# Equal token blocks in the second part of an MLP: five of 460 or 464 tokens in place of four of 512 and one of 256

## The chip, the cores and the metric

The kernel runs on one core of one Trainium2 chip. The metric is the device time of one execution in microseconds (us). The engines are TensorE (PE, with its weight loads shown apart as PEld), VectorE (DVE), ScalarE (ACT), GpSimd (POOL) and SyncE (SP, which issues the DMAs).

## The reference

Three layers follow each other over 2304 tokens (4 batches of 576) of 512 features, all in float32.

```python
x = attention(q, k, v, M_prev, z_prev, beta)       # (2304, 512), 8 heads of 64, causal, mixed with a memory read
h = x @ w_in                                       # first MLP: 512 -> 2048
g = s * relu(h)**2 + b
x = g @ w_out                                      # 2048 -> 512
h = x @ w2_in                                      # second MLP: 512 -> 1024
e = softmax(h) * h
ln = (e - mean(e)) / sqrt(var(e) + 1e-6) * g_ln
return ln @ w2_out                                 # 1024 -> 512
```

## The kernel before

**Arithmetic.** The float32 operands of the MLPs are split into a high and a low part of type fp32r, and each product of two matrices is made of three matmuls: high by high, high by low, low by high. Tokens are the moving operand in the first MLP, so the column count of a matmul is a number of tokens; the weights, 128 by 128, are the stationary operand, and each matmul has a weight load of its own.

**Stages.** The 16 groups of 128 hidden units of the first MLP (`f`, FF = 2048) are split. The first 4 groups (`FP1`) are done by `first_part`, in blocks of `NB` = 512 tokens (the last of 256), woven into the attention; its result goes to the DRAM tile `yd`. The other 12 groups (`FP2`) are done by `second_part` after the attention. The second MLP (`mlp2`) ends the kernel, 256 tokens at a time.

**second_part.** The line `blocks = ...` cuts the 2304 tokens into five blocks (t0, n). A round is one block with six of the groups: `rounds` holds the five blocks with groups 4 to 9, then the five blocks with groups 10 to 15, so ten rounds. Groups are taken two at a time, in three pairs for each round. For a pair, `hidden2` computes the hidden values with a Winograd form of the 2x2 block product: seven products (`product`, line 1098, into the PSUM tiles X, Y, V, W), each of six matmuls on m = n // 2 tokens; that is 42 matmuls of m columns for a pair and 126 for a round. Between the products ACT and DVE combine the results (lines 1123 to 1142), then `gate_of` squares and scales them on n columns (lines 1115 to 1119). `y2` (lines 1155 to 1157) multiplies by `w_out`: 12 matmuls of n columns for a group, 72 for a round; at the sixth group the sum is added into `yT` in SBUF (line 1161).

**What a round needs.** `forms2` makes the seven Winograd forms of the block, each as a high and a low tile, from x: POOL makes the differences (lines 968 to 976), ACT takes the high part (961), DVE the low part (962). There is one buffer for each form. In rounds 0 to 4 the forms are also written to the DRAM tile `fd` (line 965, 14 DMAs a round); rounds 5 to 9 read them back (line 953, 14 DMAs). `load2` brings x and the sums of `first_part` for the next round. Beside this the weights are decoded on ACT, DVE and POOL (`decode_to`), by a count of steps, three in a round.

**Order.** The program is traced loop by loop, but the order in which each engine runs its instructions is written out by hand in the dictionary `ORDER`: for each engine a list of the instructions' numbers in the order of tracing (`a+n` means n in a row from a). PE's list weaves the products of a pair with the matmuls of `y2` of the pair before, so that PE has work while the other engines handle a product. `SLOTS` names the buffer of each tile.

Of the kernel before, what the change touches and what calls it, by code (L numbers as in the profile page):

```python
# [50 lines left out]
1366+2 1428+3 1368+2 1420+8 1388+6 1387 1462 1445 1406+2 1431 1463+4 1446 1432+10 1394+4 1442+2 1398+2 1467 1447  # L51
1453+4 1448+2 1468+4 1461 1472+2 1450+3 1444 1491+12 1457 1474+2 1458 1476 1459+2 1477 1516+9 1478+7 1503+8 1485+2
1511+2 1487+4 1513+3 1540+2 1528 1525 1529 1526 1530+6 1542 1536+2 1543+2 1538+2 1545+5 1552+2 1550+2 1554+2 1527
1556+2 1564 1558 1565+4 1559 1569+2 1560+3 1571 1563 1572+9 1624 1588 1625+2 1589 1627 1636 1628+2 1637+3 1630
1640+5 1631+2 1645+2 1633 1647 1581+2 1590 1634+2 1591 1660+2 1583 1662+3 1648+2 1592 1650 1665 1584 1651 1593 1585
1594 1586+2 1652 1666 1653+2 1595+3 1600+2 1598+2 1602+9 1667 1612 1655 1613 1611 1656 1668 1614 1669 1657+3 1670
1615+2 1671+2 1617+7 1673+12 1726 1685 1720 1686+4 1696 1690+2 1697+2 1721 1692+2 1699 1694 1700+2 1695 1702+6
1722+3 1708+3 1727 1711+2 1728 1713 1729 1714+3 1725 1717+3 1730 1738+5 1744+6 1743 1731+7 1762 1768+2 1763+3 1756+5
1750 1761 1751+5 1766 1770 1767 1771+2 1774+4 1780+2 1773 1782 1778 1783 1779 1784 1789+2 1785 1791+4 1807+6 1795
1813 1796 1804+2 1814 1786 1815 1787 1797 1867 1816+5 1868 1798 1821 1799+2 1822 1801+3 1823+3 1828+2 1826 1830 1827  # L60
1831+2 1834+2 1843+2 1833 1836 1845 1837+3 1806 1861+4 1849 1858 1846 1865 1788 1840 1866 1869 1859 1841 1850 1852+6
1860 1847+2 1876 1851 1906 1842 1915+3 1894+3 1918 1907+2 1879 1873 1909 1897+2 1919 1910 1874+2 1911 1899 1870 1880
1900 1871 1885 1901+5 1920 1924 1877 1925+2 1881 1927 1966+5 1872 1878 1928 1936 1888 1929 1948+2 1937+2 1950 1939
1951+3 1940 1971 1960+2 1941 1882 1972+2 1962+2 1974 1964 1891 1975 1965 1976 1978 1892 1886+2 1883 1977 1987 1884
1889 1979 2020 1893 1890 2005 1988 2006 1980 2007 1981 2021 1989 2008+2 1982 1990 2022 1991 2010 1992 1983 2023
1933+2 2024 1912 2025 1996+4 2014 2000 2015 2001 2016+2 2026 2018 2027 2019 1935 2028 1921 2032 2029 1922 2030 2041
2031 1923 1930 1913 1931 1945 2042 1946 1957+2 1932 1914 1959 1954 1947 1955+2 1942+3 2059+2 2033+2 2061 2035 2062+2
2043 2036+2 2044+2 2064 2046 1993 2011 1994+2 2092+2 2002 2050+2 2094 2052+2 2095 2104 2054 2105 2096 2055 2106+2
2097 2047 2108 1984+2 2113 2122 2114+2 2109 2116+2 2048 1986 2003+2 2012 2056 2038 2013 2065 2039+2 2057 2066+2 2098
2058 2049 2099+5 2123 2068 2124 2069 2118 2164 2125 2165+2 2146+3 2167 2149 2126+2 2168+2 2150 2134 2151 2135+3 2070  # L70
2138+2 2158+3 2170 2161+3 2171 2176 2172+2 2177 2071 2178 2185+4 2072 2074 2174+2 2179 2075 2073 2083 2218 2076+3
2203 2079 2086 2089 2087 2090 2080 2091 2084 2088 2081 2085 2082 2180 2204 2219+4 2205+3 2181 2223 2208 2189+2
2128+2 2119+2 2212+3 2121 2194+6 2224 2215+2 2225+3 2217 2230+2 2131 2110 2228 2239 2232 2143 2132 2240+2 2233 2111
2133 2112 2130 2140 2152+3 2144 2229 2141 2155 2145 2156 2142 2157 2234 2200 2242 2191 2243 2257 2192+2 2258+2 2235
2260+2 2201+2 2244 2262 2254 2209 2248 2182 2249 2302 2183 2303 2250+3 2245 2253 2246 2290 2304 2291+2 2184 2293
2305 2311+2 2294 2313 2306 2295 2210 2314+2 2236 2255 2237+2 2296 2211 2316 2320 2256 2297 2247 2263+2 2298 2265
2321 2299 2322 2300+2 2272 2323+2 2307 2275 2266 2362 2273 2269 2325 2344 2274 2363 2345 2364 2346 2270 2347 2365
2271 2348 2366+2 2281 2332 2349 2282 2333 2267 2334 2356 2335+2 2357+2 2337 2359+2 2368+2 2268 2370+2 2361 2374+2
2276 2278 2376+2 2277 2378 2372 2287 2373 2284 2383 2379 2384 2279 2285 2385+2 2286 2401 2288 2283 2280 2387+2 2289
2308 2402 2309 2403 2326+2 2317 2410 2310 2318 2411 2328 2412 2404 2338+2 2319 2392 2341 2393 2350 2394 2340 2329  # L80
2342 2351 2343 2352 2330+2 2353+3 2395+2 2380 2397+2 2405 2416 2406 2417 2413+2 2389+2 2399 2407 2381 2415 2382 2391
2408 2400 2409 2418+28 2461 2455 2462 2452+2 2456+4 2463 2473 2467 2454 2468 2470 2446 2460 2447 2474 2471 2448 2464
2475 2449+3 2465+2 2472 2488+2 2469 2482 2485 2483 2490 2486+2 2509 2500 2510 2479 2511 2476+2 2512 2480 2484 2478
2491+2 2506+2 2501 2481 2502 2527 2493 2515 2524 2503 2513 2516 2504 2514 2517 2508 2528 2494 2525 2518 2495+5 2519
2505 2529 2520 2551 2536 2521+3 2526 2548 2560+3 2539 2530+6 2554+2 2542 2549 2552 2543+3 2572 2546+2 2563 2556 2537
2564 2557 2540 2558+2 2541 2566 2573 2567 2565 2553 2574 2568 2550 2569 2575 2538 2581 2570+2 2582+2 2614 2576
2615+2 2584+2 2599 2577 2600+2 2586 2602+2 2617 2596 2604+2 2618+2 2587 2578 2608+2 2590 2610 2591+4 2611+2 2595
2620+4 2613 2624 2579 2606 2625 2588+2 2580 2626+2 2635 2628 2636+2 2629 2638 2632 2639 2692 2653 2630 2640 2631
2654+3 2607 2659 2597 2657 2660 2693 2658 2644 2694 2633 2645+3 2641 2648+2 2642 2695 2598 2696 2634 2650 2662 2643
2697+3 2686 2700 2687 2701 2707 2688+3 2661 2691 2702 2708+3 2703 2665 2651 2716 2671 2711 2758 2652 2717 2712  # L90
2718+2 2663 2759+2 2720 2664 2740 2721 2741+4 2761 2745 2674 2752 2666 2753 2762 2668 2672 2667 2763 2677 2764 2754
2765 2755 2766+2 2728 2756 2768 2729+4 2757 2733 2769 2678+2 2669+2 2673 2779 2680 2770 2780 2681 2781 2771 2683+2
2682 2675 2685 2676 2797+2 2772 2782 2773 2799 2783+2 2713 2800 2774 2801 2775 2802 2725 2722 2704+2 2726 2714
2788+4 2818 2706 2812+2 2792 2819 2814+2 2820 2793 2816+2 2734 2715 2821 2806 2824 2807+4 2822 2737 2811 2823 2727
2749 2738 2735 2739 2723+2 2736 2833 2746 2750+2 2747+2 2825 2834 2826+3 2835 2890 2803 2836 2891 2829 2837 2851+2
2838 2853 2892 2854+2 2785 2856 2893 2776 2842+3 2777 2845+3 2896 2778 2894 2884+3 2897 2887 2794 2895 2888 2830
2898 2786 2889 2787 2795 2899+3 2804+2 2956 2839 2796 2840 2848 2957 2905 2841 2849 2958 2906 2831 2907 2850 2959+2
2914+2 2832 2857 2916 2858+2 2917 2908+2 2918 2938 2919 2910 2961 2860+2 2869 2939+2 2950 2863 2951 2941+3 2870 2952
2871 2926+2 2953 2928+4 2962 2954+2 2963+2 2864 2968+2 2965 2866 2977+2 2970 2867 2966 3010 2868 2862 2979 3011 2980
2865 3012 2971+2 2981 3013 2967 2973 3014 2878 2982 3015 2881 2995+2 2875+2 2882 2877 2872+2 3004 2997 2879+2 2883  # L100
2874 3005 2998 2902 2999 3006 2911 3007 2912 3008+2 2920 2923 3000 2903 2924 2913 2921 2925 3016+2 2986+4 3018
2990+2 2947 2935 3019 2948 3022 3020 3023 2949 3021 3031 2936+2 2922 2904 3088 3032 2944 2932+2 2945 2934 2946 3033
3089 3034+2 3090 3036 3024+2 3049+2 3026 3091 3051+4 3027 3092 2983 3001 2992 3082+4 3002 3086 3040+5 2984 3045 3094
3003 3093 3095+3 2974 3087 3098+2 2985 2975 2993 3055 2994 3056 3046+2 3037 3103+3 2976 3038 3028 3112 3154 3039
3029 3057 3030 3048 3155+2 3113 3106 3157 3114 3158 3115 3058 3136 3116 3107 3064 3117 3059 3061 3108 3137+3 3159
3060 3140 3124 3062 3125+2 3141 3067 3127+3 3148 3070 3160+2 3149+2 3162 3065 3068 3151 3166 3152+2 3163 3069 3079
3063 3175 3071 3066 3167 3073 3076 3074 3164 3208 3080 3075 3165 3072 3209 3077 3176+3 3168 3078 3081 3169 3210 3193
3179 3194 3109 3211+2 3170 3195+2 3180 3171 3121+2 3213 3197 3202+2 3198 3123 3204+4 3184+6 3100 3214+2 3101 3216
3220 3110+2 3217 3221+2 3218 3229+3 3219 3286+2 3102 3223 3118 3133 3288 3145+2 3119 3247 3120 3147 3248 3130 3289
3131 3134 3132 3135 3142+3 3232 3290 3224 3249 3233 3225 3250+2 3234 3172 3199 3291 3173 3200 3252 3201 3280+4 3174  # L110
3181 3292+2 3190 3294+2 3238+3 3284 3241 3296 3242+2 3297 3182 3285 3226 3191 3301 3227 3310 3302 3253 3303 3352+2
# [1269 lines left out]
```

## Time and profile before

| what | value |
|---|---|
| time, median of 3 runs (lowest to highest) | 807.01 us (805.99 to 808.16) |
| the profiled execution: its time, and the span in its trace | 806.04 us, 804.3 us |
| PE busy | 794.9 us (99% of the span) |
| DVE, ACT, POOL busy | 604.4, 567.7, 157.0 us |
| granted TensorE clock, mean | 0.999 |

The span runs from the first to the last instruction of the trace; the time has some 1.7 us around it. PE's busy time counts overlapping matmuls once, and the ends of matmuls are modelled, so the length of a matmul is read from the distance between the starts of neighbours and not from its duration. The times in the rows are us from the span's start, and durations of single instructions are ns where a row says mean.

### The profile page before, as it was taken

What the parts mean: (1) busy time and instruction counts of PE and PEld (TensorE: products, weight loads), DVE (VectorE), ACT (ScalarE), POOL (GpSimd) and SP (SyncE); (2) the same over time, 40 slices, a digit from 0 to 9 for tenths busy, and PEclk for the clock granted to TensorE, in tenths of its full rate; (3) what the DMA queues carried; (4) which work ended last, traced back from release to release, by engine and by line L of the source; (5) the groups of instructions that cost most, each with busy time, mean ns of one, the idle gap of its engine ahead of it and who ended that gap; (6) DMA issues with size and microseconds to landing.
All of it is one profiled execution on the core that took longest, in us unless ns stands there. A gap on an engine that the chain in (4) does not pass through costs nothing.

```text
span 804.3 us, 15061 instructions
## 1 busy us (share of the span) xinstructions
PE 794.9 (99%) x5406; PEld 666.4 (83%) x5406; DVE 604.4 (75%) x1486; ACT 567.7 (71%) x1189; POOL 157.0 (20%) x170
## 2 busy tenths in 40 slices
PE   9999999999999999999999999999999999999997
PEld 6777777877777898988899888989987888888886
DVE  6999988878789886877577579765689756766751
ACT  7999988888797669886588677765856445545542
POOL 3221232121001524221121002500012212222000
PEclk9999999999999999999999999999999999999999
DMA  8463572545766568881769867467782000001001
GB/s 262 144 206 97 161 215 80 167 151 183 253 166 189 176 214 267 279 284 52 241 236 312 290 236 261 149 233 244 242 320 90 35 13 27 28 14 40 26 14 66
DMA packets 69167, 134.02 MB, mean 167 GB/s; under 512 B 9484, under 2 KB 26596, under 8 KB 69092
## 3 DMA queue, kind: packets, MB, share of 16 engines
q1 hardware_dynamic: 69092, 133.05, 50.5%
q8 instruction: 43, 0.70, 0.4%
q14 instruction: 32, 0.26, 0.1%
HBM read 91.24 MB, written 41.79 MB: 165 GB/s over the span
## 4 chain that ended last, share of the span: by engine, by line
PE 89%; DVE 5%; ACT 3%; issue 1%; DMA 1%; POOL 1%; SPq 0%; DVEq 0%; ACTq 0%; POOLq 0%
PE y L1157 6%; PE y L1156 6%; PE y L1155 6%; PE pp L791 5%; PE W L1098 5%; PE X L1098 5%; PE V L1098 5%; PE s L734 5%; PE po L823 4%; PE o L1308 4%; PE o L1307 4%; PE o L1309 4%; PE Y L1098 2%; PE y L917 2%; PE y L919 2%; PE zt L1298 2%
## 5 line engine op out<-in xcount | busy, mean ns | idle before, releaser
L1155 PE MATMUL y<-g,w 128*128 128x512 f32 (+1 forms) x240 | 84.1, 379 | 0.0
L1156 PE MATMUL y<-g,w 128*128 128x512 f32 (+1 forms) x240 | 83.3, 376 | 0.0
L1157 PE MATMUL y<-g,w 128*128 128x512 f32 (+1 forms) x240 | 81.9, 377 | 0.0
L717 ACT ACTIVATE pr<-pr,mx 128x128 f32<-128x128 f32 (+3 forms) x128 | 71.0, 558 | 4.3 <-DVE mx L750 3.9
L795 ACT ACTIVATE pt<-pp,omg 128x512 f32<-128x512 f32 (+3 forms) x128 | 62.7, 524 | 9.6 <-PE pp L791 8.2
L750 DVE CUSTOM_DVE_ANT_0 pr<-s,big 128x256 f32<-128x256 f32 (+3 forms) x128 | 59.1, 482 | 10.4 <-PE s L734 9.2
L1098 PE MATMUL X<-fhb,w 128*128 128x256 f32 (+1 forms) x240 | 61.8, 277 | 0.0
L1098 PE MATMUL V<-fht,w 128*128 128x256 f32 (+1 forms) x240 | 61.0, 278 | 0.0
L1119 DVE TENSOR_TENSOR g<-r,g 128x512 fp32r<-128x512 f32 (+1 forms) x60 | 39.2, 654 | 22.9 <-ACT r L1118 19.2
L1307 PE MATMUL o<-w,zh 128*128 128x512 f32 x144 | 54.1, 391 | 0.0
L1117 ACT ACTIVATE g<-r,b_sb,s_sb 128x512 fp32r<-128x512 f32 (+1 forms) x60 | 45.8, 767 | 11.7 <-PE y L1157 10.4
L1308 PE MATMUL o<-w,zh 128*128 128x512 f32 x144 | 53.8, 392 | 0.0
L1309 PE MATMUL o<-w,zl 128*128 128x512 f32 x144 | 53.6, 392 | 0.0
L791 PE MATMUL pp<-ident,pr 128*128 128x128 f32 x320 | 50.1, 276 | 1.7 <-ACT pt L795 0.7
L1115 ACT ACTIVATE r<-r 128x512 f32<-128x512 f32 (+1 forms) x60 | 34.5, 582 | 22.9 <-DVE r L1138 13.2
L791 PEld LDWEIGHTS pp<-ident,pr 128*128 128x128 f32 x320 | 37.9, 140 | 13.0 <-ACT pt L795 2.1
L1157 PEld LDWEIGHTS y<-g,w 128*128 128x128 f32 x240 | 44.2, 189 | 5.0
L1156 PEld LDWEIGHTS y<-g,w 128*128 128x128 f32 x240 | 44.3, 189 | 4.6
L628 POOL TENSOR_TENSOR q<-ph,zb 128x640 f32<-128x640 f32 x16 | 25.7, 1608 | 112.1 <-DVE ph L625 86.3
L1098 PEld LDWEIGHTS X<-fhb,w 128*128 128x128 f32 x240 | 44.3, 190 | 2.8 <-ACT r L1135 0.2
L1118 ACT ACTIVATE r<-r,b_sb,s_sb 128x512 f32<-128x512 f32 (+1 forms) x60 | 45.7, 768 | 1.1
L1155 PEld LDWEIGHTS y<-g,w 128*128 128x128 f32 x240 | 43.8, 189 | 3.3
(223 smaller groups left out, 2414.0 us busy)
## 6 DMA issues: line engine op xcount, KB each, us to landing
raw<-in_moe_w_in_dram SPq DMA_DIRECT2D x24, 512.0 KB, 5.7
raw<-in_moe_w_out_dram SPq DMA_DIRECT2D x24, 512.0 KB, 4.3
wd<-wt SPq DMA_DIRECT2D x21, 512.0 KB, 3.1
w<-wd SPq DMA_DIRECT2D x21, 512.0 KB, 4.7
kq<-in_kq_dram SPq DMA_DIRECT2D x16, 608.0 KB, 5.6
RW<-rd SPq DMA_DIRECT2D x24, 288.0 KB, 5.0
q<-in_q_dram SPq DMA_DIRECT2D x16, 320.0 KB, 3.8
v<-in_v_dram SPq DMA_DIRECT2D x16, 320.0 KB, 5.3
```

The lines of the kernel that those rows point to most:

```text
L717: mark[0] = nc.scalar.activation(pr, pr, AF.Exp, bias=mx, scale=-1.0, accum_out=sm).ins
L750: nc.vector.tensor_tensor_reduce(pr, ss[:, j, at[i]:at[i] + n], big[:, CF * P - i * P:CF * P - i * P + n], -scale, FMAX, ALU.add, ALU.min, mx)
L791: nc.tensor.transpose(pp[:, e * n + c * P:e * n + (c + 1) * P], pr[:, c * P:(c + 1) * P], ident)
L795: nc.scalar.activation(p["pt", i // 2][:, j, 0:i + 1, i % 2, :], pp[:, e * n:(e + 1) * n].rearrange("p (c t) -> p c t", t=P), AF.Copy, sca ...
L1098: nc.tensor.matmul(o, wc[a], b[:, i, 0:m], start=(i == 0 and z == 0 and not more), stop=(i == KH - 1 and z == 2), skip_group_check=True)
L1117: nc.scalar.activation(gh, r, AF.Identity, scale=s_sb, bias=b_sb)
L1155: nc.tensor.matmul(o, wc[0], gh, start=(f == fs[0]), stop=False)
L1156: nc.tensor.matmul(o, wc[1], gh, start=False, stop=False)
L1157: nc.tensor.matmul(o, wc[0], gl, start=False, stop=(f == fs[-1]))
L1307: nc.tensor.matmul(oo, zh, w[:, 0], start=(f == 0), stop=False)
L1308: nc.tensor.matmul(oo, zh, w[:, 1], start=False, stop=False)
L1309: nc.tensor.matmul(oo, zl, w[:, 0], start=False, stop=(f == NF2 - 1))
```

## The change

The five blocks of `second_part` become four of 460 tokens and one of 464, where they were 512, 512, 512, 256 and 512. The half blocks, which are the columns of the matmuls of `product`, become 230 or 232, where they were 256 (or 128 in the block of 256 tokens). Nothing else in the program's loops is changed: the number of instructions of each kind stays as it is, and so do the blocks of `first_part`.

```diff
-    blocks = [(0, NB), (NB, NB), (2 * NB, NB), (3 * NB, NT - 4 * NB), (NT - NB, NB)]
+    BT = NT // 5 // 4 * 4
+    blocks = [(i * BT, BT if i < 4 else NT - 4 * BT) for i in range(5)]
```

The lists of `ORDER` are also replaced in part. They hold the same numbers as before. PE's list has 4654 entries: the first 1405 and the last 730 are unchanged, and of those between some 1500 stand more than 5 places from where they stood, the farthest 84. ACT's list has 1008 entries (farthest 55 places), DVE's 1272 (40), SP's 382 (19) and POOL's 170 (4). Two lines of PE's list, as a sample of the kind of change:

```diff
-1366+2 1428+3 1368+2 1420+8 1388+6 1387 1462 1445 1406+2 1431 1463+4 1446 1432+10 1394+4 1442+2 1398+2 1467 1447
...
+1366+2 1428+2 1368 1430 1369 1431 1420+8 1388+6 1462 1387 1463 1445 1464 1406+2 1465+2 1446 1394+2 1432+2 1396+2
...
```

## Rows read from the trace of the kernel before

**Rows 1.** Page, parts 1, 2 and 4: busy time, granted clock by slices, chain that ended last
```profile
PE 794.9 (99%) x5406; PEld 666.4 (83%) x5406; DVE 604.4 (75%) x1486; ACT 567.7 (71%) x1189; POOL 157.0 (20%) x170
...
PEclk9999999999999999999999999999999999999999
...
PE 89%; DVE 5%; ACT 3%; issue 1%; DMA 1%; POOL 1%; SPq 0%; DVEq 0%; ACTq 0%; POOLq 0%
```

**Rows 2.** Windows, second_part: stretch, its length, busy us (x instructions) of each engine, clock, DMA
```profile
289.70:602.00 312.30, 311.57 (x2038) 281.67 (x2037) 223.47 (x445) 225.80 (x411) 55.43 (x52) 1.00 0.72 241
```

**Rows 3.** Windows, the same stretch, instructions of line 1098 alone: PE busy, PEld busy
```profile
289.70:602.00 312.30, 196.62 (x1260) 181.85 (x1260) 1.00 0.72 241
```

**Rows 4.** Groups of instructions by shape: xcount, busy us, mean ns of one, idle before
```profile
L1098 PE MATMUL X<-fhb,w 128*128 128x256 f32 x192 | 50.9, 282 | 0.0
...
L1098 PE MATMUL X<-fhb,w 128*128 128x128 f32 x48 | 10.8, 254 | 0.0
...
L1155 PE MATMUL y<-g,w 128*128 128x512 f32 x192 | 71.4, 401 | 0.0
```

**Rows 5.** Timeline of PE, 256 columns, two apart: start, duration, line, names, stationary, moving, count
```profile
300.06 0.28 PE L1098 MATMUL Y<-fht,w 128*128 128x256 f32 x1
...
300.30 0.28 PE L1098 MATMUL Y<-fht,w 128*128 128x256 f32 x1
```

**Rows 6.** Windows, the longest stretch of 256-column matmuls alone
```profile
559.72:580.30 20.58, 20.58 (x170) 20.32 (x170) 12.17 (x28) 15.74 (x30) 0.00 (x0) 1.00 0.72 237
```

**Rows 7.** Timeline of PE, stretch of 128 columns alone: first and last, 12 apart
```profile
403.94 0.28 PE L1098 MATMUL Y<-fht,w 128*128 128x128 f32 x1
...
405.29 0.27 PE L1098 MATMUL W<-fht,wh 128*128 128x128 f32 x1
```

**Rows 8.** Timeline of PE, two matmuls of 128 columns among 512-column ones
```profile
379.83 0.44 PE L1156 MATMUL y<-g,w 128*128 128x512 f32 x1
380.12 0.22 PE L1098 MATMUL W<-fht,wh 128*128 128x128 f32 x1
380.18 0.27 PE L1098 MATMUL W<-flt,wh 128*128 128x128 f32 x1
380.29 0.45 PE L1155 MATMUL y<-g,w 128*128 128x512 f32 x1
380.57 0.62 PE L1156 MATMUL y<-g,w 128*128 128x512 f32 x2
```

**Rows 9.** Timeline of PEld, the weight loads in the same stretch
```profile
380.12 0.19 PEld L1098 LDWEIGHTS W<-flt,wh 128*128 128x128 f32 x1
380.23 0.19 PEld L1155 LDWEIGHTS y<-g,w 128*128 128x128 f32 x1
380.34 0.42 PEld L1156 LDWEIGHTS y<-g,w 128*128 128x128 f32 x2
```

**Rows 10.** Timeline of PE, 512 columns in second_part: first and next after four
```profile
371.88 0.39 PE L1157 MATMUL y<-g,w 128*128 128x512 f32 x1
...
372.80 0.28 PE L1098 MATMUL W<-flt,wh 128*128 128x256 f32 x1
```

**Rows 11.** Waits of PE in second_part: who waited for whom, us in total, times, longest
```profile
PE Y L1098 <- DVE flt L962: 0.4, 1, 0.4
PE W L1098 <- DVE r L1132: 0.2, 1, 0.2
```

**Rows 12.** Timeline of PE where round 1 begins
```profile
319.65 0.40 PE L1155 MATMUL y<-g,w 128*128 128x512 f32 x1
320.45 0.38 PE L1098 MATMUL Y<-flt,w 128*128 128x256 f32 x1 [0.40 <-DVE flt L962]
```

**Rows 13.** Groups of ACT in second_part by shape, the gate's line 1117
```profile
L1117 ACT ACTIVATE g<-r,b_sb,s_sb 128x512 fp32r<-128x512 f32 x48 | 38.6, 810 | 6.6 <-PE y L1157 5.9
...
L1117 ACT ACTIVATE g<-r,b_sb,s_sb 128x256 fp32r<-128x256 f32 x12 | 7.2, 596 | 5.1 <-PE y L1157 4.4 <-PE V L1098 0.6
```

**Rows 14.** Windows, round 1 of second_part, columns as in rows 2
```profile
318.70:350.00 31.30, 30.76 (x192) 27.00 (x191) 24.78 (x45) 26.51 (x47) 10.23 (x9) 1.00 0.77 266
```

337 rows, old and new, of the table ORDER are left out of this document.

## The prediction

> **What bounds the kernel.** I read the page first, then windows, then the timeline of PE. The page has PE busy for 99% of the span and on 89% of the chain that ended last, at the full granted clock in every slice (2.4 GHz, the higher of its two levels) [rows 1]. So the time is PE's instruction stream, and an edit counts by what it does to that stream. The window over `second_part`, 312.3 us, says the same of the stage that is changed: PE is busy 311.57 us, DVE 223, ACT 226, DMA at 0.72 [rows 2]. PE waited for another engine 0.6 us in all [rows 11]. What must be known, then, is how long PE takes for a matmul of each width. Durations don't tell (254, 282 and 401 ns for 128, 256 and 512 columns [rows 4], since neighbours overlap); the distances of starts do.
>
> **Prices of a matmul.** With 256 columns, starts stand 120 ns apart [rows 5], and in the longest stretch of that width alone 20.58 us / 170 = 121 ns [rows 6]. I take 121. With 512 columns four steps take 0.92 us: 230 ns [rows 10]. With 128 columns twelve steps take 1.35 us: 112.5 ns [rows 7]. From 512 to 256 the price falls by 109 ns, or 0.426 ns a column; from 256 to 128 it falls by only 8.5. So below some width something else sets the step. Rows 8 and 9 show what. Two matmuls of 128 columns follow one of 512: the second is taken up 60 ns after the first (380.12 to 380.18), because its stream is that short, but the next then stands 110 ns on (380.29), and a 512-column matmul behind it is followed after 280 ns and not after 230. The weight loads run through at 380.12, 380.23 and 380.34, 110 ns apart, whatever the width [rows 9]. A narrow matmul thus waits for the load of the next weights; about 112 ns is a floor for each matmul with a load of its own.
>
> The Trainium skill (TensorE: Matmul & The Clock Gate, section LDWEIGHTS) gives a load of P columns P / 1.2 ns, 106.7 ns for 128 columns; the 110 ns in rows 9 bear the floor out, a little higher. By the page's figure the floor would lie under the stream of 230 columns, the stream would set the step, and the saving worked out below would be an estimated 10 us.
>
> **Removed and added on PE.** Counts first. Line 1098 has 1260 matmuls in the stage [rows 3]; the groups show 192 to 48 for the two widths [rows 4], so 1008 of 256 columns and 252 of 128. `y2` has 720: 576 of 512 and 144 of 256. A check of the prices: 1008 x 0.121 + 252 x 0.1125 = 150.3 us, and 576 x 0.230 + 144 x 0.121 = 149.9 us. PE ran 2038 matmuls in the stretch; the other 58 belong to the neighbouring stages, at 0.121 to 0.230 us another 7 to 13 us. The sum, 307 to 313, is the stage's 312.3.
>
> *Products.* After the change all 1260 have 230 columns (252 of them 232). No row has that width. The line through 256 and 512 columns gives 121 - 26 x 0.426 = 110 ns, under the floor of 112.5, so I take 112.5: 1260 x 0.1125 = 141.8 us, against 150.3: **-8.6 us**. The bounds: 109 ns if the stream alone set the step and the floor gave way (with the 256-column price at 122, a saving of 14); upward, the load and the stream are then nearly as long as each other, and each could delay the other as they run together; the 256-column price itself, 121, is the end, 1260 x 0.121 = 152.5, +2.1 us. The nearest row is the floor's, since 110 lies below it.
>
> *y2.* The number of matmuls and the sum of their columns stay the same, and the price is a line between 256 and 512, so 720 matmuls of 460 or 464 columns cost 149.9 again. If the price went in proportion to columns under 512 (0.230 / 512 x 460 = 207 ns, against 208 on the line) it would be 0.9 us less. I take **0**.
>
> **Beside PE.** ACT and DVE do the same number of operations on the same sum of elements. Line 1117 shows the form of their price: 810 ns at 512, 596 at 256 [rows 13], so a part that doesn't change with width and 0.84 ns a column; at 460 a gate's operation takes some 766 ns. The total is unchanged, 226 us of ACT now in about 304. In the fullest round, round 1, ACT is busy 26.5 of 31.3 us [rows 14]; that round becomes about 29.1 us of PE (126 x 0.1125 + 72 x 0.208), and ACT's work falls less, by about 5% where it depends on the width, so its share goes from 85% to about 88%. It is not the bound, but it has less slack there; the round with 256 tokens gives up the slack it had. The weight decoding goes by steps, three a round, and so is spread more evenly in time. The 14 writes and 14 reads of forms a round keep their number and their bytes over the stage; rows 11 name no DMA as something PE waited for, so I cost them at nothing. What hides them is the three pairs between a form's last use and its next, and if that cover failed, the loss would be at the round's start, where it is priced below.
>
> *The new order.* PE's list is rewoven through the whole stage. Its cost could be below zero (the 0.6 us of waits could go) or above. The nearest row is the start of round 1: from 319.65 to 320.45 is 0.80 us where a 512-column matmul takes 0.23, so 0.57 us lost while DVE makes a form's low part [rows 12]. If each of the nine round starts lost as much, that is 9 x 0.57 = 5.1, 4.5 more than now. The forms shrink by a tenth with the matmuls that cover them, so I take **0**, and keep -0.6 to +4.5 for the range.
>
> **Sum.** -8.6 + 0 + 0. The profiled execution took 806.04 us with a span of 804.3; it becomes 797.4, the span 795.7. The median of the runs lies 0.97 above that execution, so I predict 807.01 - 8.6 = **798.4 us**.
>
> **Rivals.**
> 1. *Load and stream hinder each other.* At 230 columns both take about 110 ns. With the step half-way between floor and 256-column price, 116.8 ns, 1260 matmuls take 147.2: -3.1, 803.9 us. With the full 121, +2.1: 809.1. For it: 256 columns cost 121 where the load needs 110, so a stream that fully overlaps a load already pays something. Against: 512 columns, with the same overlap, lie on a plausible line.
> 2. *No floor.* If a matmul cost its columns plus a constant at every width, the same count and the same columns would cost the same: 0, 807.0 us. For it: the 60 ns between the first two starts in rows 8. Against: 112.5 ns over twelve in a row [rows 7]. The Trainium skill (same page, Back-to-back issue gap) has such a rule, N / 2.4 + 2.5 ns for a matmul by itself; the trace differs from it at 128 columns, 112.5 against 55.8, and the measurement decides.
> 3. *Half rate under 256 columns: slower.* The 112.5 ns could be the matmul's own stream, run at 0.88 ns a column because it is narrower than 256. Then 230 columns take 202 ns, 1260 x 0.202 = 254.5, +104: 911 us. It turns against the change from 150.3 / 1260 = 119.3 ns for each matmul. Against: the second start 60 ns after the first and the loads' even 110 [rows 8, 9].
> 4. *Waits at the round starts: slower or nothing gained.* Forms come late after a rewoven order, because ACT has less slack in rounds 0 to 4. At 0.57 us for each of nine starts the result is -4.1; to eat the gain it takes 0.96 us a start, and beyond 1.2 the kernel is measurably slower, about 810. Against: one such stop in the present trace, not nine.
>
> **Chances.** Forecast (floor, within 3 us) 0.70; rival 1 half-way 0.12; rival 1 in full 0.06; rival 2 0.02; rival 3 0.04; rival 4 0.06, of which 0.04 measurably slower. A measurement of this kernel can tell 0.3%, 2.4 us, from no change. Faster than 804.6: 0.82; within: 0.06 + 0.02 + 0.02 = 0.10; slower: 0.08. For the range: down to 794.0 (most of the 14 us of the lower bound), up to 804.0 (rival 1 half-way, or the round starts at 0.57); this leaves out what is left of rivals 1 to 4.
>
> **What would show it.** In the changed kernel's timeline of PE, runs of 230-column matmuls should step by 112 ns and 460-column ones by 208; the window of the stage should be 303 to 304 us with PE still busy throughout, and PE's waits for ACT and DVE about 1 us. The attention and the second MLP should keep their lengths (290 and 202 us). A step of 117 or more, a stage that is shorter only on paper because waits of several us appear beside the matmuls, or a gain in another stage would make the reasoning wrong.

## The result

The changed kernel takes 800.34 us (median of 4 runs, 799.28 to 800.88), the kernel before 807.59 us (median of 4, 805.99 to 809.18): a ratio of 0.9909 with a 95% interval of 0.9885 to 0.9933, some 7.3 us less. 798.4 us had been forecast, 8.6 us less, in a range of 794.0 to 804.0.

The page of the changed kernel, parts 1, 3 and 4, beside [rows 1]; part 3's line with the packets is the one that changed most:

```profile
PE 787.1 (99%) x5406; PEld 669.9 (84%) x5406; DVE 600.8 (75%) x1486; ACT 567.3 (71%) x1189; POOL 154.7 (19%) x170
...
DMA packets 83502, 134.00 MB, mean 168 GB/s; under 512 B 9484, under 2 KB 59364, under 8 KB 83428
...
PE 78%; DVE 9%; DMA 5%; ACT 4%; issue 2%; SPq 1%; POOL 0%; DVEq 0%; ACTq 0%; POOLq 0%
```

PE is still busy for 99% of a span that is now 798.3 us (the execution took 800.85). Of the chain that ended last, DVE and DMA hold 9% and 5% of the span, where they held 5% and 1%.

Windows of the changed kernel: before its first product in `second_part`, from there to its last matmul of `y2`, and after. Columns are the length, busy time (x instructions) of PE, PEld, DVE, ACT, POOL, then clock and DMA.

```profile
0.00:290.60 290.60, 286.82 (x2438) 222.82 (x2439) 249.69 (x752) 245.90 (x609) 64.65 (x72) 1.00 0.56 174
290.60:596.30 305.70, 303.65 (x2040) 285.45 (x2039) 223.61 (x450) 227.78 (x415) 54.24 (x52) 1.00 0.75 245
596.30:798.30 202.00, 196.58 (x932) 161.58 (x930) 127.53 (x286) 93.64 (x166) 35.77 (x46) 1.00 0.11 42
```

The middle row answers to [rows 2]. Cut in the same way, at the first product (289.7) and the last `y2` (602.1), the stage was 312.4 us before and is 305.7 now: 6.7 us less. The stage ahead of it is 0.9 us longer, the second MLP 0.2 shorter; together that is the 6.0 us by which the spans differ. DVE and ACT are as busy in the stage as they were.

The timeline of PE, where runs of one width begin and end (first row and the row after the last): 30 matmuls of 230 columns, then 18 of 460.

```profile
319.08 0.27 PE L1100 MATMUL V<-fht,w 128*128 128x230 f32 x1
...
322.46 0.38 PE L1158 MATMUL y<-g,w 128*128 128x460 f32 x1
...
400.27 0.38 PE L1158 MATMUL y<-g,w 128*128 128x460 f32 x1
...
404.01 0.27 PE L1100 MATMUL W<-fht,wh 128*128 128x232 f32 x1
```

That is 3.38 us / 30 = 112.7 ns for a product and 3.74 / 18 = 207.8 ns for a matmul of `y2`; 112.5 and 208 had been taken. (Before, products were line 1098 and `y2` lines 1155 to 1157; now 1100 and 1157 to 1159.)

What PE waited for in the stage, beside [rows 11]; columns: who waited for whom, us in total, times, longest:

```profile
PE V L1100 <- ACT yo L922: 0.9, 1, 0.9
PE V L1100 <- DVE u L1131: 0.6, 1, 0.6
PE W L1100 <- DMA flt<-fd: 0.3, 1, 0.3
PE X L1100 <- ACT r L1137: 0.2, 1, 0.2
```

2.0 us in place of 0.6. Both of the long ones lie in round 0.

### The profile page after: what moved, and what is told of

Its sections match the earlier page's. It is cut to its first block, busy times and chain, and to the rows that moved or that the text cites. A ratio compares the mean times of both kernels' runs of the same rounds, so it can differ in the third digit from the quotient of the medians.

```text
span 798.3 us, 15056 instructions
## 1 busy us (share of the span) xinstructions
PE 787.1 (99%) x5406; PEld 669.9 (84%) x5406; DVE 600.8 (75%) x1486; ACT 567.3 (71%) x1189; POOL 154.7 (19%) x170
## 2 busy tenths in 40 slices
DMA packets 83502, 134.00 MB, mean 168 GB/s; under 512 B 9484, under 2 KB 59364, under 8 KB 83428
## 4 chain that ended last, share of the span: by engine, by line
PE 78%; DVE 9%; DMA 5%; ACT 4%; issue 2%; SPq 1%; POOL 0%; DVEq 0%; ACTq 0%; POOLq 0%
PE y L1158 6%; PE y L1159 6%; PE y L1157 6%; PE W L1100 5%; PE V L1100 5%; PE X L1100 4%; PE o L1310 4%; PE o L1311 4%; PE o L1309 4%; PE pp L792 4%; PE s L735 3%; PE po L824 2%; PE Y L1100 2%; PE zt L1300 2%; PE h L855 2%
## 5 line engine op out<-in xcount | busy, mean ns | idle before, releaser
L1158 PE MATMUL y<-g,w 128*128 128x460 f32 (+1 forms) x240 | 80.4, 370 | 0.0
L1157 PE MATMUL y<-g,w 128*128 128x460 f32 (+1 forms) x240 | 78.3, 371 | 0.0
L1159 PE MATMUL y<-g,w 128*128 128x460 f32 (+1 forms) x240 | 77.8, 370 | 0.0
L1100 PE MATMUL V<-fht,w 128*128 128x230 f32 (+1 forms) x240 | 61.3, 277 | 1.5 <-ACT yo L922 0.9
L1100 PE MATMUL X<-fhb,w 128*128 128x230 f32 (+1 forms) x240 | 61.4, 275 | 0.2 <-ACT r L1137 0.2
L1121 DVE TENSOR_TENSOR g<-r,g 128x460 fp32r<-128x460 f32 (+1 forms) x60 | 40.4, 675 | 23.1 <-ACT r L1120 22.8
L1117 ACT ACTIVATE r<-r 128x460 f32<-128x460 f32 (+1 forms) x60 | 34.7, 584 | 30.4 <-DVE r L1144 18.2
L1119 ACT ACTIVATE g<-r,b_sb,s_sb 128x460 fp32r<-128x460 f32 (+1 forms) x60 | 45.4, 767 | 4.2 <-PE y L1159 3.0
L1158 PEld LDWEIGHTS y<-g,w 128*128 128x128 f32 x240 | 44.9, 189 | 4.1
L1159 PEld LDWEIGHTS y<-g,w 128*128 128x128 f32 x240 | 44.8, 189 | 3.9
L1157 PEld LDWEIGHTS y<-g,w 128*128 128x128 f32 x240 | 44.3, 189 | 4.0
L629 POOL TENSOR_TENSOR q<-ph,zb 128x640 f32<-128x640 f32 x16 | 25.7, 1608 | 112.7 <-DVE ph L626 86.6
L1100 PEld LDWEIGHTS V<-fht,w 128*128 128x128 f32 x240 | 44.1, 191 | 3.1 <-DVE u L1131 1.1
L735 PE MATMUL s<-kq 64*128 64x128 f32 x640 | 46.1, 286 | 0.6 <-DVE sm L773 0.4
```

The source lines that it names most:

```text
L735: self.last = nc.tensor.matmul(ss[:, j, c0 + k * P:c0 + (k + 1) * P], x[:, S + i * P:S + (i + 1) * P], x[:, k * P:(k + 1) * P], start=True ...
L1100: nc.tensor.matmul(o, wc[a], b[:, i, 0:m], start=(i == 0 and z == 0 and not more), stop=(i == KH - 1 and z == 2), skip_group_check=True)
L1157: nc.tensor.matmul(o, wc[0], gh, start=(f == fs[0]), stop=False)
L1158: nc.tensor.matmul(o, wc[1], gh, start=False, stop=False)
L1159: nc.tensor.matmul(o, wc[0], gl, start=False, stop=(f == fs[-1]))
```

## The experiments

Two questions were put to runs: whether the width of the matmuls alone brings the gain (A) or the rewoven order does (B); and whether the price of a narrow matmul is a floor set by the weight load, a half rate under 256 columns, or its columns plus a constant. The runs with blocks of 400 or 512 tokens and the run of widths were made once each. Executions of the kernel before spread from 804.9 to 808.4 us on one chip, so a microsecond or two between single runs, or between delays read from one execution each, shows nothing.

For the comparison each stage is split into its own matmuls at a price, its neighbours' matmuls, and what is left, called delay. The price is a line through the steps of the fourth run below: 13.5 ns + n / 2.4 for n columns, and never under 111.8 ns. At 230, 256, 460 and 512 columns it lies within 1.5 ns of the steps of that run. The delays that stand in the expectations were counted a little differently and are 0.6 to 1.1 us higher.

### Blocks and order apart

The first run takes the new blocks with the old lists, the second the old blocks with the new lists.

```diff
 # first: the changed kernel
-ORDER = { ... the rewoven lists ... }
+ORDER = { ... the lists of the kernel before ... }
 # second: the changed kernel with its lists, and
-    BT = NT // 5 // 4 * 4
-    blocks = [(i * BT, BT if i < 4 else NT - 4 * BT) for i in range(5)]
+    blocks = [(0, NB), (NB, NB), (2 * NB, NB), (3 * NB, NT - 4 * NB), (NT - NB, NB)]
```

> The five equal blocks of the change with the written-out order of the kernel before. Theory A (the gain is the width of the matmuls alone, 1260 products at the weight-load floor in place of 1008 wide ones and 252 narrow ones): 7 to 9 us below the kernel before, about 799 us, since the order was good for nothing but hiding other engines. Theory B (the gain comes from the rewoven order): about 807 us, no difference. If the rewoven order is needed for the new widths, the PE waits of this run add up to several us more than the 3.8 us of single delays seen in the stage after the change, and the time lies between 799 and 807.

> The blocks of the kernel before (512, 512, 512, 256, 512) with the rewoven order of the change. Theory A: no gain, 807 us, or up to 3 us slower where the order fits the other widths. Theory B: most of the 7 us gained, about 800 us.

New blocks with the old order: 806.28 us against 806.04 for the kernel before on the same chip, ratio 0.9994 (0.9983 to 1.0006), no gain at all. Old blocks with the new order: 815.56 us, ratio 1.0120 (1.0105 to 1.0135), slower. So neither A nor B holds: alone, one half of the change gives nothing and the other costs 9.5 us, and together they give 7. What came is the last case of the first expectation, that the new widths need the new order; PE's waits in the stage were 3.9 us in that run and 2.0 in the changed kernel. Windows of their stages:

```profile
288.60:602.60 314.00, 309.56 (x2037) 285.32 (x2037) 223.76 (x446) 226.10 (x411) 53.43 (x52) 0.99 0.75 240
```

```profile
290.10:610.90 320.80, 313.87 (x2040) 285.37 (x2039) 224.05 (x450) 227.97 (x415) 55.13 (x52) 0.99 0.69 232
```

Split as said above (us; the neighbours' matmuls are 9.0 with the old lists and 9.4 with the new). The last column adds up what the weight loads of the stage (PEld) waited for other engines and DMAs:

| kernel | stage | own matmuls at the price | delay | waits of weight loads |
|---|---|---|---|---|
| before | 312.4 | 297.3 | 6.1 | 5.3 |
| changed | 305.7 | 288.8 | 7.5 | 4.0 |
| new blocks, old order | 314.0 | 288.8 | 16.2 | 12.4 |
| old blocks, new order | 320.8 | 297.3 | 14.1 | 9.6 |

By this price the own matmuls fall by 8.4 us with the blocks, whatever the order. An order that doesn't fit gives all of it back as delay. In each of the last two rows 1.7 us of the delay is a fall of TensorE's clock (last section); of what is left of the rise, 8.4 and 6.3 us, the weight loads' longer waits make up most (7.1 and 4.3 us more than before). The first line of these waits in the stage, with the old order on the new blocks:

```profile
PEld W L1099 <- DVE r L1133: 5.5, 13, 0.8
```

and the same wait in the kernel before and in the changed one:

```profile
PEld W L1098 <- DVE r L1132: 3.1, 12, 0.6
```

```profile
PEld W L1100 <- DVE r L1134: 0.8, 4, 0.2
```

W has one buffer: DVE reads the sum of the fourth product from it, then the sixth product adds to it. The wait was there before, 3.1 us beside PE's other work; with narrower matmuls and the old list it grew to 5.5; with the new list it is nearly gone. It is spread over the rounds, and so is the delay: 0.9 to 1.6 us in every round but round 8. That one, which was the second round of 256 tokens, has 4.8 us; there the forms come late from DRAM, and the fall of the clock follows. Timeline of PE, the matmul before the longest wait and the one that waited:

```profile
524.56 0.38 PE L1157 MATMUL y<-g,w 128*128 128x460 f32 x1
...
526.12 0.35 PE L1099 MATMUL X<-fhb,w 128*128 128x230 f32 x1 [1.18 <-DMA fhb<-fd]
```

With the old blocks and the new order, 4.5 and 6.0 us of the delay lie in rounds 4 and 9 (in round 9 with the fall of the clock), the ones that follow a round of 256 tokens; that fits new lists that make no allowance for such a round.

Whether PE's list alone would do, with the old lists elsewhere, wasn't tried, since the lists hang on one another.

### Columns taken away: five blocks of 400

```diff
-    blocks = [(i * BT, BT if i < 4 else NT - 4 * BT) for i in range(5)]
+    blocks = [(i * BT, 400) for i in range(5)]
...
```

> The changed kernel with five blocks of 400 tokens, so that 304 tokens get no second part (left out; all their other work stays). The products have 200 columns in place of 230, y2 has 400 in place of 460. Floor theory: the 1260 products keep their step of 112 to 113 ns and give nothing; y2 gives 720 x 60 x 0.426 ns = 18.4 us; 782 us. If a product cost its columns (0.43 to 0.48 ns each), another 16 to 18 us would go: 764 to 766 us.

(In lines not shown here, the load of the first part's sums still covers all tokens.)

780.4 us, 782 expected from the floor and 764 to 766 from a price by columns. The products went from 230 to 200 columns and gave nothing: in rows of products alone the median step from start to start is 111 ns, and 112 at 230 columns. What went, some 20 us, is `y2`'s 18.2 us at the price and 1.5 of delay.

### The price of a width by itself

A kernel of matmuls only, 40 in a row of each width, accumulating eight at a time.

```diff
+    def series(n, count=40, rows=P):
+        for k in range(count):
+            t = ps[(k // 8) % 4]
+            c = (k % 4) * P
+            nc.tensor.matmul(t[0:rows, 0:n], sta[:, c:c + rows], mov[:, 0:n], start=(k % 8 == 0), stop=(k % 8 == 7))
...
```

> Only matmuls of the products' type, 40 in a row for each width, with nothing beside them (the attention and both MLPs are left out). Floor theory: with 128 columns of weights the step is 107 to 112 ns at 64, 128, 176, 200, 216, 224 and 230 columns, then rises by 0.42 to 0.43 ns a column (256: 117 to 121, 512: 227 to 230); with 64 columns of weights the floor is about half, 55 ns, up to 96 columns, and 230 columns then cost 98 to 110 ns. Half rate under 256 columns: the step grows by 0.83 ns a column from 128 to 244 (230: 200 ns) and falls back at 256, and the 64-column weights change nothing. Columns plus a constant: 64 columns 30 to 40 ns, 128 columns 56 ns.

Groups by shape of that kernel; stationary (128*128 or 128*64 weights), moving, count, busy us, mean ns of one:

```profile
L37 PE MATMUL ps<-mov,sta 128*128 128x128 f32 x40 | 8.8, 416 | 0.0
L37 PE MATMUL ps<-mov,sta 128*128 128x176 f32 x40 | 8.8, 416 | 0.0
L37 PE MATMUL ps<-mov,sta 128*128 128x460 f32 x40 | 8.4, 368 | 0.0
...
L37 PE MATMUL ps<-mov,sta 128*128 128x256 f32 x40 | 5.0, 284 | 0.0
...
L37 PE MATMUL ps<-mov,sta 128*128 128x216 f32 x40 | 4.6, 275 | 0.0
L37 PE MATMUL ps<-mov,sta 128*128 128x230 f32 x40 | 4.6, 275 | 0.0
L37 PE MATMUL ps<-mov,sta 128*128 128x236 f32 x40 | 4.6, 275 | 0.0
...
L37 PE MATMUL ps<-mov,sta 128*64 128x230 f32 x40 | 4.4, 270 | 0.0
...
L37 PE MATMUL ps<-mov,sta 128*64 128x160 f32 x40 | 3.1, 236 | 0.0
...
L37 PE MATMUL ps<-mov,sta 128*64 128x32 f32 x40 | 2.5, 209 | 0.0
```

Busy time less the duration of the last one, over 39, is the step. The rows round the busy time to 0.1 us, so the steps here are taken from the starts in the same trace. With 128 columns of weights the step is 111.8 ns at 216, at 230 and at 236 columns alike, 120.0 at 256 and 206.7 at 460: a floor, and above it (206.7 - 120.0) / 204 columns = 0.42 ns a column. With 64 columns of weights 230 columns take 106.7 ns, 160 take 73.7 and 32 take 57.5, far under the 111.8: the floor is the load's and shrinks with it. Half rate under 256 columns (200 ns at 230) is out.

So are columns plus a constant, which would have made it 30 to 40 ns at 64 columns: the starts of that series stand 109 ns apart in the mean until the granted clock falls to its lower level (last section). At that level the steps double, and there is a floor too: 214 ns at 128 and at 176 columns alike.

### The same orders on other widths

Why does the old order lose on equal blocks? One theory (C): narrower matmuls bring PE back to a buffer sooner, while the operations of DVE and ACT shrink less. The other (D): its lists were woven around the round of 256 tokens and lose wherever that round is another. Each order was run with five blocks of 512 (overlapping by 64, so 256 tokens are done twice) and the old one also with five of 400. (In lines not shown below, the first part's sums are loaded once where blocks overlap.)

```diff
-    blocks = [(i * BT, BT if i < 4 else NT - 4 * BT) for i in range(5)]
+    blocks = [(i * 448, NB) for i in range(5)]
...
```

> The old order with five overlapping blocks of 512 tokens (256 tokens are done twice, so the sums of those are doubled): every round has the width for which most of the old lists were written. Delay here means the time of the stage less its matmuls at max(111.8, 13.5 + n / 2.4) ns each; it was 6.7 us before, 8.5 after, 17.1 with the old order on 460 tokens. Theory C (narrower matmuls bring PE back sooner to a buffer that DVE or ACT still reads, and their operations shrink less): the delay falls to 5 to 8 us, time 823 to 826 us (matmuls +19 us). Theory D (the old lists lose wherever the blocks differ from 512, 512, 512, 256, 512, because rounds 3 and 8 were woven for 256 tokens): delay 12 us or more, most of it in rounds 3, 4, 8 and 9, time over 830 us.

> The new order with the same five overlapping blocks of 512 tokens (256 tokens done twice). Theory C: wider matmuls leave more time for the others, delay 5 to 9 us as with 460, time 825 to 829 us. Theory D': the new lists fit only their own widths, delay 12 us or more, over 831 us.

> The old order with five blocks of 400 tokens (304 tokens get no second part). The new order had 7.1 us of delay at this width and 780.4 us. Theory C: the old order loses more than at 460, where it had 17.1: delay 19 to 25 us, time 790 to 796 us. Theory D: as at 460, 17 us, time 788 us.

826.58, 818.94 and 787.65 us. Delay in the stage, us:

| five blocks of | 400 | 460 or 464 | 512 |
|---|---|---|---|
| old order | 14.7 | 16.2 | 9.6 |
| new order | 6.0 | 7.5 | 2.3 |

The weight loads' waits go with it: 12.9, 12.4 and 9.2 us with the old order, 3.2, 4.0 and 0.8 with the new.

The windows of the stages of the two at 512, old and new:

```profile
289.40:622.70 333.30, 331.08 (x2038) 292.70 (x2038) 234.20 (x446) 239.30 (x411) 58.06 (x52) 1.00 0.70 239
```

```profile
288.20:614.60 326.40, 326.31 (x2040) 294.79 (x2039) 234.36 (x450) 240.66 (x415) 58.49 (x52) 1.00 0.71 241
```

C is right in direction from 460 to 512: both orders lose 5 to 7 us less when the matmuls are wider, the old one not quite as little as expected, the new one less (818.94 us where 825 to 829 had been expected). It missed at 400: the delay of the old order didn't grow (without the fall of the clock it would be 14.5 at 460, against 14.7), and 787.65 us is what D had named, 788. That fits the floor too: under 236 columns the products of PE stop shrinking, while DVE's operations go on shrinking (line 1128 on the tile Y, 397 ns at 230 columns in the first row below, from the changed kernel, and 365 at 200 in the second, from the run with blocks of 400). That this is the reason C missed was not tested further.

```profile
L1128 DVE TENSOR_TENSOR u<-Y,u 128x230 f32<-128x230 f32 x24 | 9.5, 397 | 12.9 <-ACT u L1125 6.9 <-PE Y L1100 4.2 <-ACT wh L513 1.1
```

```profile
L1129 DVE TENSOR_TENSOR u<-Y,u 128x200 f32<-128x200 f32 x30 | 11.0, 365 | 16.4 <-ACT u L1126 10.4 <-PE Y L1101 4.4 <-ACT wh L513 1.0
```

D missed at 512, where it had over 830 us, and explains only part: with equal blocks of each of the three widths the old order loses 7 to 9 us more than the new, at 400 and 512 spread over all rounds but the first, at 460 half of it in round 8. The new lists are better for equal blocks of each width. Which of their moves does it stays open.

### The wait at the start of round 0

ACT copies the last results of `first_part` into two tiles, and waited there for the DMA that empties them; PE waited for that copy. Timeline of ACT in the changed kernel:

```profile
298.40 0.38 ACT L922 ACTIVATE yo<-y 128x256 f32<-128x256 f32 x1 [1.08 <-DMA yd<-yo]
```

A third tile:

```diff
-        ys = Slots(fctx.enter_context(tc.tile_pool(name="ys", bufs=1)), "ys.", 2)
+        ys = Slots(fctx.enter_context(tc.tile_pool(name="ys", bufs=1)), "ys.", 3)
-    'ys.y': '01011010010010101011',
+    'ys.y': '01201201201201201201',
```

> The changed kernel with three buffers in place of two for the result tiles of the first part, so that ACT need not wait for a DMA before it copies the last of them; PE waited 0.88 us for that copy at the start of round 0, 1.04 us in all at this place. If that wait goes and nothing else is late there, 0.9 us is gained on the changed kernel: ratio to the kernel before 0.990 where the changed kernel had 0.9909. If something else is next (the product's own inputs, or DVE), nothing is gained.

799.8 us, ratio 0.9918 (0.9893 to 0.9944), the changed kernel's 0.9909 within the interval. The wait is gone and the stage is 1.4 us shorter in the profiled execution (304.3), its delay 6.1:

```profile
290.60:594.90 304.30, 303.47 (x2040) 285.48 (x2039) 223.28 (x450) 227.56 (x415) 54.23 (x52) 1.00 0.76 246
```

The last stage took 203.9 us there and not 202.0. PE's part of it was no longer (197.6 us to its last matmul, 197.7 in the changed kernel); the difference came after it, while the output was written. Whether the 0.9 us are gained can't be told: the interval holds 0.990 and 0.9909 alike, and the six executions spread from 797.4 to 803.5 us.

## Why the prediction was right, and where it was not

**The price of a product: right.** 112.5 ns was taken for 230 columns; 112.7 was found in the stage and 111.8 in the run with nothing beside it. The floor belongs to the weight load, as [rows 8] and [rows 9] had suggested, and the load and the stream do not hinder each other: 230 columns cost what 216 do. Rivals 1, 2 and 3 fall with the run of widths; rival 2, the plain constant, also with the blocks of 400. The Trainium skill's figure for a load of 128 columns (TensorE: Matmul & The Clock Gate, section LDWEIGHTS), 106.7 ns, is some 5 ns under the step that the runs show.

**The counts and `y2`: right.** By the straight-line price the own matmuls of the stage fell by 8.4 us, with 8.6 forecast, and `y2` by nothing. That `y2` keeps its cost is then a property of the line; with the steps that were measured at 256, 460 and 512 columns in its place, `y2` gets 0.6 us dearer and the fall is 7.6 us.

**The order: costed at 0, measured at +0.5 to +1.4, and not where the range had looked for it.** The delay of the stage rose from 6.1 to 7.5 us, or by 0.5 with the measured steps, inside the -0.6 to +4.5 that had been left open and no more than executions of one kernel differ by. The stage took 305.7 us where 303 to 304 had been forecast. The rise did not come at nine round starts: round 0 went from 0.7 to 2.8 us of delay, two stops make 1.8 us of that, and the other nine rounds together lost less than before (4.6 us, 5.5 before). PE's waits for ACT and DVE came to 1.7 us where about 1 had been forecast. Timeline of PE, the matmul ahead of each and the one that waited:

```profile
297.68 0.27 PE L1100 MATMUL X<-flb,w 128*128 128x230 f32 x1
298.83 0.38 PE L1100 MATMUL V<-fht,w 128*128 128x230 f32 x1 [0.88 <-ACT yo L922]
...
313.47 0.27 PE L1100 MATMUL X<-flb,w 128*128 128x230 f32 x1
314.36 0.38 PE L1100 MATMUL V<-fht,w 128*128 128x230 f32 x1 [0.62 <-DVE u L1131]
```

**What the working missed** is the size of what the order hides. Rival 4 asked whether the new lists would make forms come late; the danger lay on the other side. The old lists on the new widths lose 10 us more than on their own, which is more than the change brings, and [rows 11], with 0.6 us of PE's waits, could not show how little room was behind them. The weight loads' waits of the kernel before, 5.3 us, were in the same trace and showed some of it. The prediction was right because the lists were rewoven with the blocks; for the blocks alone the same working would have forecast 798 us, and 806 was measured. To that extent the 0 for the order was luck: the working had nothing that tells a list that fits from one that doesn't.

**Smaller misses.** The DMAs kept their number and bytes, but not their packets: 83502, where there were 69167, those under 2 KB more than twice as many; that fits forms of 230 columns which no longer fill their tiles of 256 and so go in two pieces (14 DMAs in each of the eight rounds that had 512 tokens, over 128 partitions, are 14336 pieces more; the page has 14335). PE waited once for the DMA of a form, 0.3 us. And the stage ahead of the change ended 0.9 us later, which no step had allowed for; in the other runs of the kernel it ended anywhere from 288.2 to 290.6 us, so this may be scatter.

## What to carry to other kernels

A matmul can't be made cheaper by making it narrower than its weight load; so cut the moving side into equal blocks near or above that width (here some 236 columns for 128 columns of weights), and avoid a small remainder, which pays the floor on few columns. Below that width count by matmuls, not by columns. And where the order of the engines is written out by hand, widths and order are one change: measured apart, each may look useless or harmful.

## What the runs showed of the hardware that was not expected

**A wait can cost more than its length: the clock fell after it.** In the profiled executions of the new blocks with the old order and of the old blocks with the new order, the granted clock of TensorE left its full level after PE had waited. Windows of the new blocks with the old order, right after PE had waited for two DMAs (0.38 and 1.18 us) within 2 us:

```profile
522.00:528.00 6.00, 4.43 (x28) 3.72 (x27) 2.99 (x6) 3.17 (x8) 0.00 (x0) 0.89 0.98 303
528.00:534.00 6.00, 6.00 (x34) 5.65 (x34) 3.01 (x6) 4.02 (x8) 0.00 (x0) 0.82 0.82 293
```

and of the old blocks with the new order, after one wait of 2.0 us:

```profile
568.00 0.28 PE L1158 MATMUL y<-g,w 128*128 128x256 f32 x1
...
570.28 0.39 PE L1099 MATMUL V<-fht,w 128*128 128x256 f32 x1 [2.00 <-DVE u L1130]
```

```profile
570.00:576.00 6.00, 5.72 (x35) 5.73 (x36) 2.92 (x7) 2.79 (x6) 0.00 (x0) 0.72 0.34 113
```

A mean of 0.72 over 6 us, at levels of 1.0 and 0.5 (2.4 and 1.2 GHz), is 3.4 us at the lower level and 1.7 us of work lost, nearly as much again as the wait. It doesn't come in every execution: the other eleven of the first kernel had a mean clock of 0.999 or 1.0, where this one had 0.997, and two of the second's four had 1.0. That the waits brought the fall is argued from these two places.

**The clock also fell during narrow matmuls in a row, without a wait of PE.** In the kernel of widths the clock went to its lower level late in the series of 64 columns, after 512-column matmuls at the full one, and stayed there through those of 128 and 176 and most of 200; from 216 on it was full again. It was at its lower level again from 121.1 to 128.0 us, during the series of 64, 96 and 128 columns with 64 columns of weights. Windows where the series of 64 columns ends, inside that of 128, and among those of 216 to 236:

```profile
27.00:30.00 3.00, 3.00 (x25) 3.00 (x24) 0.00 (x0) 0.00 (x0) 0.00 (x0) 0.83 0.00 0
...
33.00:36.00 3.00, 3.00 (x16) 3.00 (x15) 0.00 (x0) 0.00 (x0) 0.00 (x0) 0.50 0.00 0
...
60.00:63.00 3.00, 3.00 (x29) 3.00 (x29) 0.00 (x0) 0.00 (x0) 0.00 (x0) 1.00 0.00 0
```

In the kernel before, the 252 products of 128 columns stood among wider ones, and the clock stayed at 0.999.

**DVE was slow beside POOL.** The second stop in round 0 came with one DVE operation that took 1.53 us, where its like take 676 ns in the mean, while POOL worked on a form. Rows of POOL, of DVE and of the group:

```profile
312.32 1.17 POOL L971 TENSOR_TENSOR xr<-xr 128x460 f32<-128x460 f32 x1
```

```profile
312.46 1.53 DVE L1121 TENSOR_TENSOR g<-r,g 128x460 fp32r<-128x460 f32 x1 [0.30 <-ACT r L1120]
```

```profile
L1121 DVE TENSOR_TENSOR g<-r,g 128x460 fp32r<-128x460 f32 x48 | 32.4, 676 | 11.2 <-ACT r L1120 10.9
```

The trace tells more of these 48: the 38 with no POOL operation beside them took 621 to 641 ns. Of the ten with one beside them six took no longer, and four took 868, 984, 1183 and 1534 ns. DVE's operations on PSUM tiles (line 1128, 396 ns beside POOL and 398 without) were not slower. In the run with three tiles the same place took 1534 ns again. So the slow ones all stood beside POOL; why only some did is open, and no run took POOL's work away.
